# Blocked mirroring of rows, an in-place residual and a new instruction order in a linear-attention, Fourier-mixing and feed-forward kernel

## The chip, the cores and the metric

The kernel runs on one core of one Trainium2 chip. The metric is device time in microseconds (us) of one execution; less is better. TensorE is called PE below, VectorE DVE, ScalarE ACT, GpSimd POOL and SyncE SP; SP computes nothing here and only issues transfers. A time is the median of the executions listed, with the lowest and highest in brackets.

## The reference

The input is 8 batches of 8 heads, 576 rows and 64 columns per head. Each batch goes through a linear attention with exponential features, a two-dimensional Fourier transform of which the real part is kept and added, a layer norm and a feed-forward network (FFN).

```python
def phi(x):                                   # w_phi: 64 x 128
    proj = np.einsum('bhsd,df->bhsf', x, w_phi)
    proj = proj - np.max(np.abs(proj), axis=-1, keepdims=True)
    return np.concatenate([np.exp(proj), np.exp(-proj)], axis=-1)
q_p, k_p = (phi(q), phi(k))
kv = np.einsum('bhsf,bhsd->bhfd', k_p, v)
z = np.sum(k_p, axis=2)
num = np.einsum('bhsf,bhfd->bhsd', q_p, kv)
den = np.einsum('bhsf,bhf->bhs', q_p, z)[..., None] + 1e-06
# attention output num / den, heads side by side: x is (8, 576, 512)
...
mixed = np.real(np.fft.fft(np.fft.fft(x, axis=1), axis=2))
u = x + mixed
un = (u - mu) / np.sqrt(var + 1e-06)          # over the 512 columns
out = u + np.maximum(un @ w_ch1, 0.0) @ w_ch2 # 512 -> 2048 -> 512, float32
```

## The kernel before

The real part of the transform of row s and column c equals the one of the mirrored row 576 - s and the mirrored column, so the kernel computes half of the rows and adds each product twice, once mirrored. For that it keeps a batch in five row groups on the 128 partitions: groups 0 and 1 hold rows 1 to 256 in pairs, groups 2 and 3 hold rows 320 to 575 **mirrored**, and group 4 holds rows 0 and 257 to 319. The mirrored groups must be stored in reversed order of rows. Before the change, the reversal is within blocks of 64 partitions:

```python
def out_rows(b, c):
    if c < 2:
        r = out[b, 1:257, :].rearrange("(a r j) n -> a r j n", r=64, j=2)[:, :, c, :]
        return [(slice(64, 128), r[0]), (slice(0, 64), r[1])]
    r = out[b, 320:576, :].rearrange("(a r j) n -> a r j n", r=64, j=2)
    return [(slice(0, 128), r[:, ::-1, 3 - c, :])]

def forward(b):
    ...                                        # 32 steps of the first FFN matrix, then:
    for c in range(4):
        ...                                    # 16 matmuls into po
        O = outp.tile([128, C], F32, tag="O", name="O")       # two such buffers
        nc.vector.scalar_tensor_tensor(
            out=O[:], in0=po[:], scalar=rs[:, c:c + 1], in1=U[:, c, 0:C],
            op0=ALU.mult, op1=ALU.add,
        )
        for ps_, rows_ in out_rows(b, c):
            nc.sync.dma_start(out=rows_, in_=O[ps_, :])
        yield
    ...                                        # group 4: a third and a fourth use of O
```

The loads are issued from POOL, the transposes (done by transfers) and the stores from SP, one after another (in one period of the profile before, Q's transposes from 301.4 us, a store at 309.9, K's transposes at 312.4):

```python
def turn_k(KS, KS4):
    ...
    for g in range(2):
        nc.sync.dma_start_transpose(
            out=KT[:, 8 * g:8 * g + 8, :],
            in_=KS[:, 4 * g:4 * g + 4, :].rearrange("p h x -> p (h x)"),
        )
    nc.sync.dma_start_transpose(out=KT4[:], in_=KS4[:].rearrange("p h d -> p (h d)"))
    return KT, KT4

def fetch_k(b):
    turned_k[b] = turn_k(*load_k(b))           # load and transposes in one step
    yield
```

The order of instructions is written by hand as a string. Each letter takes one step of one generator: F the FFN of batch b; M, D, N the heads and mixing, folding and normalising of batch b+1; P, T, R, S query maxima, key and query features, key maxima and scaling of the values of batch b+2; K and V its loads; Q and A the load and the transposes of Q of batch b+3. A letter whose condition is not yet met is held and tried again at each later letter.

```python
PERIOD = (
    "FFMFMFPMPFMPFKMFPMPFMFFVMMMFFFTMFFFMTFFFMRFFFMFFMFFFPFMTDMFFTFSFFTFRFFFF"
    "TDFFNFRMSFFMMTFRMMSTTFFFQTFSTRFFNTFNTAFMFFFTFTFFTNFFFTTFTFNFFFF"
)
...
weave(START, P=P, T=T, R=R, S=S_)              # features of batch 0
staged[1] = load_q(1)
load_ffn_weights()
arrive_1 = arrive(1)                           # transposes of Q of batch 1
next(arrive_1)
for b in range(-1, B):
    ...
    weave(PERIOD if b >= 0 else FIRST, **streams)
```

Of the kernel before, what the change touches and what calls it, by code (L numbers as in the profile page):

```python
# [9 lines left out]
AT = mybir.ActivationFunctionType  # L10
# [10 lines left out]
START = "STTPTRTRTTSSTRTRTRPSSPTTTTPPTTTTPT"  # L21
FIRST = "MMMPMPMMPMKMMMMMPTSTTRTRSVSMTMTRPMPTTTTSMRRTTDTMNSNTQDTTNMMMMNTTMANMTTTT"
PERIOD = (
    "FFMFMFPMPFMPFKMFPMPFMFFVMMMFFFTMFFFMTFFFMRFFFMFFMFFFPFMTDMFFTFSFFTFRFFFF"
    "TDFFNFRMSFFMMTFRMMSTTFFFQTFSTRFFNTFNTAFMFFFTFTFFTNFFFTTFTFNFFFF"
)
# [8 lines left out]
def kernel(  # L35
# [10 lines left out]
    nc = tc.nc  # L46
# [21 lines left out]
    outp = ctx.enter_context(tc.tile_pool(name="outp", bufs=2))  # L68
# [21 lines left out]
    def load_ffn_weights():  # L90
        nc.gpsimd.dma_start(out=W1b[:], in_=moe_w_ch1.rearrange("(j p) h -> p j h", p=128))
        nc.gpsimd.dma_start(out=W2b[:], in_=moe_w_ch2.rearrange("(j p) c -> p j c", p=128))

# [5 lines left out]
    TURN = const.tile([128, 128], F32, name="TURN")  # L99
# [10 lines left out]
    def count():  # L110
        nc.gpsimd.iota(pc_i[:, 0:1], pattern=[[1, 1]], base=0, channel_multiplier=1)
        for g in range(2):
            nc.gpsimd.iota(
                pc_i[64 * g:64 * g + 64, 1:2], pattern=[[1, 1]],
                base=129 - 128 * g, channel_multiplier=2,
            )
        nc.gpsimd.iota(rc_i, pattern=[[1, C]], base=0, channel_multiplier=0)

    def generate_constants():
# [13 lines left out]
        for j in range(2):  # L133
            for a in range(2):
                nc.vector.tensor_scalar(
                    out=rs[:, 128 * j + 64 * a:128 * j + 64 * a + 64], in0=rc[:, 0:64],
                    scalar1=2.0, scalar2=float(129 - 128 * a + j), op0=ALU.mult, op1=ALU.add,
                )
# [32 lines left out]
    def fix_constants():  # L171
# [7 lines left out]
        tn = gi[:, 3, 0:128].bitcast(F32)  # L179
        nc.gpsimd.iota(  # L180
            rc_i[:, 0:128], pattern=[[1, 128]], base=0, channel_multiplier=1
        )
        nc.vector.tensor_copy(out=tn, in_=rc_i[:, 0:128])
        nc.vector.tensor_single_scalar(out=TURN[:], in_=tn, scalar=63.0, op=ALU.is_equal)
        nc.vector.scalar_tensor_tensor(
            out=TURN[:], in0=tn, scalar=191.0, in1=TURN[:], op0=ALU.is_equal, op1=ALU.add
        )
# [25 lines left out]
    def load_q(b):  # L213
# [3 lines left out]
        for g in range(2):  # L217
            nc.gpsimd.dma_start(
                out=QS01[64 - 64 * g:128 - 64 * g],
                in_=q[b, :, 1 + 128 * g:129 + 128 * g, :].rearrange(  # L220
                    "h (p j) d -> p h (j d)", j=2
                ),
            )
        nc.gpsimd.dma_start(
            out=QS23[:], in_=q[b, :, 320:576, :].rearrange("h (p j) d -> p h (j d)", j=2)
        )
# [44 lines left out]
    def features(b):  # L271
# [115 lines left out]
        def weigh_q():  # L387
            pt = pk.tile([128, H, 2], F32, tag="pk", name="pt")
            nc.tensor.matmul(pt[:], lhsT=TURN[:], rhs=mq[:, :, 2:4], start=True, stop=True)
            nc.scalar.activation(  # L390
                out=E2[:, :, 0:2], in_=mq[:, :, 0:2], func=AT.Exp, scale=2.0
            )
            nc.scalar.activation(
                out=E2[:, :, 4:5], in_=mq[:, :, 4:5], func=AT.Exp, scale=2.0
            )
            nc.scalar.activation(out=E2[:, :, 2:4], in_=pt[:], func=AT.Exp, scale=2.0)
# [16 lines left out]
        def queries(t, g):  # L413
            QT = (QT01, QT23)[t]
            psh = pj.tile([128, 2, 4, 128], F32, tag="pj", name="psh")
            for jj in range(2):
                rr = slice(64 * jj, 64 * jj + 64)
                rq = QT[rr, 4 * g:4 * g + 4, :]
                if t:
                    rq = rq.rearrange("p h (a r) -> p (h a) r", r=64)[:, :, ::-1]  # L420
# [228 lines left out]
    def out_rows(b, c):  # L649
        if c < 2:  # L650
            r = out[b, 1:257, :].rearrange("(a r j) n -> a r j n", r=64, j=2)[:, :, c, :]
            return [(slice(64, 128), r[0]), (slice(0, 64), r[1])]
        r = out[b, 320:576, :].rearrange("(a r j) n -> a r j n", r=64, j=2)
        return [(slice(0, 128), r[:, ::-1, 3 - c, :])]

    def forward(b):
# [15 lines left out]
        for c in range(4):  # L672
            po = pb.tile([128, C], F32, tag="pb", name="pso")
            for hh in range(NHH):
# [6 lines left out]
            O = outp.tile([128, C], F32, tag="O", name="O")  # L681
            nc.vector.scalar_tensor_tensor(  # L682
                out=O[:], in0=po[:], scalar=rs[:, c:c + 1], in1=U[:, c, 0:C],
                op0=ALU.mult, op1=ALU.add,
            )
            for ps_, rows_ in out_rows(b, c):
                nc.sync.dma_start(out=rows_, in_=O[ps_, :])
            yield
        po = pb.tile([128, C], F32, tag="pb", name="pso")
        for hh in range(NHH):  # L690
# [7 lines left out]
        O = outp.tile([128, C], F32, tag="O", name="O")  # L698
        nc.vector.scalar_tensor_tensor(
            out=O[0:64, :], in0=po[0:64, :], scalar=rs[0:64, 4:5], in1=U[0:64, 4, 0:C],  # L700
            op0=ALU.mult, op1=ALU.add,
        )
        nc.vector.scalar_tensor_tensor(
            out=O[0:64, :], in0=po[64:128, :], scalar=rs[0:64, 4:5], in1=O[0:64, :],
            op0=ALU.mult, op1=ALU.add,
        )
        nc.sync.dma_start(out=out[b, 257:320, :], in_=O[1:64, :])
        nc.sync.dma_start(out=out[b, 0:1, :], in_=O[0:1, :])
        yield


    staged = {}

    def fetch_q(b):
        staged[b] = load_q(b)
        yield

    def arrive(b):
        turned_q[b] = turn_q(*staged.pop(b))
        yield  # L720

    def fetch_k(b):
        turned_k[b] = turn_k(*load_k(b))
        yield

    def fetch_v(b):
        values[b] = load_v(b)
        yield

    def fold_later(b):  # L730
        yield from folds[b]
# [7 lines left out]

    NEEDS = {  # L740
        "D": lambda i, n: n("M") >= 15 + i,
        "M": lambda i, n: n("D") >= 2 if i >= 16 else True,
        "N": lambda i, n: n("M") >= (21, 21, 22, 22, 23, 23)[min(i, 5)],
        "T": lambda i, n: n("K") >= 1 and n("M") >= (8 if i < 9 else 16),
        "R": lambda i, n: n("T") >= (2 * i + 1 if i < 4 else 9),
        "S": lambda i, n: n("V") >= 1 and n("R") >= min(i + 1, 5) and n("M") >= 8,
        "Q": lambda i, n: True,
        "A": lambda i, n: n("Q") >= 1 and n("T") >= 18 and n("P") >= 6,
    }

    def weave(plan, **streams):
        done = {}
        live = dict(streams)

        def count_of(name):
            return done.get(name, 0) if name in streams else 1000

        def step(name):
            if name not in live:
                return True  # L760
            if name in NEEDS and not NEEDS[name](done.get(name, 0), count_of):
                return False
            try:
                next(live[name])
                done[name] = done.get(name, 0) + 1
            except StopIteration:
                del live[name]
                done[name] = 1000
            return True

        held = []
# [4 lines left out]
        while live:  # L776
            for name in list(live):
                step(name)

    with tc.manual_schedule():  # L780
        count()
        turned_k[0] = turn_k(*load_k(0))
# [57 lines left out]
```

## Time and profile before

| | before |
|---|---|
| time | 594.2 us (592.3 to 595.4) |
| span of the profiled execution | 590.6 us |
| busy: PE, DVE, ACT, POOL | 71%, 57%, 50%, 46% |
| first FFN matmul | 118.9 us |
| one period in the middle (between starts of Q's transposes) | 64.3 to 66.0 us |
| last stretch (last sum of a full row group to the end) | 12.2 us |

A period here is one batch through all stages, woven with its neighbours, so the time is about the fill plus some five periods plus the last batches, which have less and less beside them.

### The profile page before, as it was taken

The numbers are of one execution on the slowest core, as the hardware profiler recorded it, in microseconds if no ns is written. First come the engines' busy times: TensorE is split into PE (matmuls) and PEld (weight loads), VectorE is DVE, ScalarE is ACT, GpSimd is POOL, SyncE is SP. The second block draws the span as 40 slices with busy tenths as digits, with TensorE's granted clock in tenths as the row PEclk, the third lists the DMA queues.
The fourth block names the chain that finished last, engine by engine and source line by source line (L and its number), as shares of the span: only waits on it lengthen the run. The fifth ranks groups of instructions, "written<-read, shape, count | busy, mean of one in ns | idle before, by whom it ended". The sixth has DMA issues, their size and how long they took to land.

```text
span 590.6 us, 9983 instructions
## 1 busy us (share of the span) xinstructions
PE 422.1 (71%) x3881; PEld 255.2 (43%) x3904; DVE 338.5 (57%) x621; ACT 296.1 (50%) x644; POOL 273.0 (46%) x351
## 2 busy tenths in 40 slices
PE   0231442598897689759984989658967988999892
PEld 0111430177345553546443743535335734854651
DVE  7740476566766378437764577528844675557111
ACT  2771055347673468337653667336743766631520
POOL 8191079247662365518661566336651753441000
PEclk9999999989998799879998799979997899999897
DMA  9749950691199307990499009930799007006111
GB/s 115 89 43 180 191 75 0 66 150 28 21 110 152 42 9 97 143 75 2 50 136 123 15 19 105 152 48 1 93 120 111 2 22 74 27 18 70 35 36 44
DMA packets 115806, 42.66 MB, mean 72 GB/s; under 512 B 92080, under 2 KB 110640, under 8 KB 115760
## 3 DMA queue, kind: packets, MB, share of 16 engines
q1 hardware_dynamic: 63504, 23.67, 34.5%
q0 software_dynamic: 52256, 18.37, 29.0%
q8 instruction: 30, 0.49, 0.4%
q14 instruction: 16, 0.13, 0.1%
HBM read 36.77 MB, written 9.44 MB: 78 GB/s over the span
## 4 chain that ended last, share of the span: by engine, by line
DMA 32%; PE 29%; DVE 22%; POOL 6%; ACT 4%; issue 4%; SPq 2%; DVEq 0%; POOLq 0%; ACTq 0%
DMA KT<-KS 13%; DMA QT<-QS 12%; PE pso L675 10%; PE psf L663 8%; DMA out_dram<-O 4%; POOL FEO L467 3%; DVE MK L346 3%; DVE SE L480 2%; PE psD L578 2%; DVE st L628 2%; PE pu L600 2%; DVE cb L528 2%; DMA KS<-in_k_dram 2%; POOL X L531 2%; DVE MQ L383 2%
## 5 line engine op out<-in xcount | busy, mean ns | idle before, releaser
L663 PE MATMUL psf<-UT,W1b 128*128 128x288 bf16 x1024 | 158.1, 304 | 13.4 <-DMA UT<-UN 6.9
L668 ACT ACTIVATE HT<-psf 128x288 bf16<-128x288 f32 x256 | 104.4, 413 | 98.4 <-PE psf L663 90.3
L675 PE MATMUL pso<-W2b,HT 128*128 128x512 bf16 x490 | 119.8, 380 | 2.1 <-issue 1.9
L663 PEld LDWEIGHTS <-W1b 128*128 128x128 bf16 x1024 | 98.2, 104 | 45.8 <-issue 17.9
L531 POOL TENSOR_TENSOR X<-cb,rd 128x320 f32<-128x320 f32 x64 | 46.2, 722 | 151.4 <-DVE rd L530 150.8
L675 PEld LDWEIGHTS <-HT 128*128 128x128 bf16 x512 | 44.9, 98 | 55.6 <-issue 10.2
L383 DVE TENSOR_REDUCE MQ<-psq 128x8 f32<-128x1024 f32 x32 | 38.4, 1222 | 49.3 <-PE psq L376 49.3
L305 POOL TENSOR_TENSOR VCn<-VS,VCn 128x512 bf16<-128x512 bf16 x32 | 34.1, 1065 | 50.4 <-ACT VCn L301 46.6
L467 POOL TENSOR_TENSOR FEO<-X 128x320 f32<-128x320 f32 x64 | 55.4, 886 | 2.5
L330 PE MATMUL psk<-wphi,KT 64*128 64x128 bf16 x256 | 15.5, 253 | 55.0 <-DMA KT<-KS 48.5
L336 ACT ACTIVATE KPp<-psk 128x1024 bf16<-128x1024 f32 x32 | 32.9, 1029 | 43.3 <-PE psk L330 42.4
L346 DVE TENSOR_REDUCE MK<-psk 128x8 f32<-128x1024 f32 x32 | 38.7, 1210 | 18.3 <-ACT KPp L336 12.3
L376 PE MATMUL psq<-wphi,QT 64*128 64x128 bf16 x256 | 15.3, 250 | 46.2 <-DMA QT<-QS 42.3
L509 ACT CAST kvh<-kv 128x130 bf16<-128x130 f32 x64 | 17.2, 268 | 46.0 <-PE kv L505 45.0
L682 DVE SCALAR_TENSOR_TENSOR O<-pso,rs,X 128x512 f32<-128x512 f32 x32 | 23.7, 739 | 27.6 <-PE pso L675 27.6
L430 ACT ACTIVATE QPHP<-psh 128x1024 bf16<-128x1024 f32 x32 | 32.8, 1026 | 7.5 <-PE psh L421 7.5
L336 ACT ACTIVATE KPn<-psk 128x1024 bf16<-128x1024 f32 x32 | 33.1, 1035 | 6.4 <-DVE MK L346 6.4
L330 PEld LDWEIGHTS <-KT 64*128 64x128 bf16 x256 | 9.3, 108 | 61.6 <-DMA KT<-KS 50.6
L305 POOL TENSOR_TENSOR VCp<-VS,VCp 128x512 bf16<-128x512 bf16 x32 | 34.4, 1074 | 0.0
L430 ACT ACTIVATE QPHN<-psh 128x1024 bf16<-128x1024 f32 x32 | 32.8, 1026 | 0.0
L642 POOL TENSOR_SCALAR VE<-MV 128x5 f32<-128x5 f32 x8 | 4.1, 515 | 62.0 <-DVE MV L629 62.0
L376 PEld LDWEIGHTS <-QT 64*128 64x128 bf16 x256 | 8.9, 106 | 52.3 <-DMA QT<-QS 45.0
(389 smaller groups left out, 803.3 us busy)
## 6 DMA issues: line engine op xcount, KB each, us to landing
KS<-in_k_dram POOLq DMA_DIRECT2D x16, 256.0 KB, 6.7
VS<-in_v_dram POOLq DMA_DIRECT2D x8, 512.0 KB, 15.8
out_dram<-O SPq DMA_DIRECT2D x32, 128.0 KB
out_dram<-O SPq DMA_DIRECT2D x16, 256.0 KB
QS<-in_q_dram POOLq DMA_DIRECT2D x16, 128.0 KB, 3.4
QS<-in_q_dram POOLq DMA_DIRECT2D x8, 256.0 KB, 6.2
W1b<-in_moe_w_ch_dram POOLq DMA_DIRECT2D x1, 2048.0 KB, 16.1
W2b<-in_moe_w_ch_dram POOLq DMA_DIRECT2D x1, 2048.0 KB, 28.3
```

The costliest lines, as they stand in the source:

```text
L305: nc.gpsimd.tensor_tensor(out=VC[:, hs, :, 0:D], in0=values[b][0][:, hs, :].rearrange("p h (j d) -> p h j d", d=D), in1=VC[:, hs, :, D:D + ...
L330: nc.tensor.matmul(psk[:, jj, x, :], lhsT=turned_k[b][0][rr, 4 * pr + x, :], rhs=wphi2[rr, :], start=True, stop=True,)
L336: nc.scalar.activation(out=KP[:, hs, :, :].rearrange("p e (jp jj) f -> p jj (e jp) f", jj=2), in_=psk[:], func=AT.Exp, scale=sgn,)
L346: nc.vector.tensor_reduce(out=MK[:, 2 * pr:2 * pr + 2, :].rearrange("p e (jp jj) -> p jj (e jp)", jj=2), in_=tiles[pr][:], axis=AX.X, op=A ...
L376: nc.tensor.matmul(psq[:, jj, x, :], lhsT=QT[rr, 4 * g + x, :], rhs=wphi2[rr, :], start=True, stop=True,)
L383: nc.vector.tensor_reduce(out=mv_, in_=psq[:], axis=AX.X, op=ALU.max, apply_absolute_value=True)
L430: nc.scalar.activation(out=o, in_=psh[:], func=AT.Exp, scale=sgn)
L467: nc.gpsimd.tensor_tensor(out=FEO[:, :, i, a:a + D], in0=X[:, :, a:a + D], in1=X[:, :, C - a:C - a - D:-1], op=op,)
L531: nc.gpsimd.tensor_tensor(out=X[:, :, D * h:D * h + D], in0=cb[:, :, 0:D], in1=rd[:].to_broadcast([128, 5, D]), op=ALU.mult,)
L663: nc.tensor.matmul(ps[:], lhsT=W1b[:, cc, 128 * hh:128 * hh + 128], rhs=UT[:, cc, 288 * hf:288 * hf + 288], start=(cc == 0), stop=(cc == N ...
L668: nc.scalar.activation(out=HT[:, hh, 288 * hf:288 * hf + 288], in_=ps[:], func=AT.Relu)
L675: nc.tensor.matmul(po[:], lhsT=HT[:, hh, 128 * c:128 * c + 128], rhs=W2b[:, hh, :], start=(hh == 0), stop=(hh == NHH - 1),)
```

## The change

Its intent has four parts. The mirrored groups are reversed in blocks of 32 rows, so that their stores have four blocks as the outermost dimension, in place of two. The residual sum is written back over the tile X that holds it and is stored from there, so the output buffers fall away. The load of K and its transposes become two streams (K and B). And the order of all steps is new, with the start, the weights (W) and all batches in one plan, and conditions that count steps per batch.

```diff
-START = "STTPTRTRTTSSTRTRTRPSSPTTTTPPTTTTPT"
-FIRST = "MMMPMPMMPMKMMMMMPTSTTRTRSVSMTMTRPMPTTTTSMRRTTDTMNSNTQDTTNMMMMNTTMANMTTTT"
-PERIOD = (...)
+START = "TTTRTRSRTTRQSRSPTAPTTTTTPTSPPSKTTTPTMMTPMMTPWMMMPTMWTMRMTMTSPMRTTMPTMSNNDMTRPNSSMTRVRTSQBMAMMDMMTMTNTTTNTTMN"
+PERIOD = "MFMFMKRFMPVFMPFFPMFPFPMFMMFFMFMFFMTFFMFFMFBFPFFMRFFFFTFMFDFTFSSFTFSTFFFFMFQFDFFTFMFFMFRMTTFMNTTRTFFMFFFFTNFSNTTFFFRFFNATFNFTSTFFTFFNFMFFFF"
...
-    outp = ctx.enter_context(tc.tile_pool(name="outp", bufs=2))
...
-        for g in range(2):
+        for QS, at in ((QS01, 1), (QS23, 320)):
             nc.gpsimd.dma_start(
-                out=QS01[64 - 64 * g:128 - 64 * g], ...
+                out=QS[:], in_=q[b, :, at:at + 256, :].rearrange("h (p j) d -> p h (j d)", j=2)
             )
... (constants and the small product that turns the maxima, for blocks of 32)
-    def out_rows(b, c): ...
+    def store(b, U, c):
+        if c == 1:
+            for a in range(4):
+                nc.sync.dma_start(
+                    out=out[b, 193 - 64 * a:257 - 64 * a, :].rearrange("(r j) n -> r j n", j=2),
+                    in_=U[32 * a:32 * a + 32, 0:2, 0:C],
+                )
+        elif c in (2, 3):
+            rows_ = out[b, 320:576, :].rearrange("(a r j) n -> a r j n", r=32, j=2)
+            nc.sync.dma_start(out=rows_[:, ::-1, 3 - c, :], in_=U[:, c, 0:C])
...
-            O = outp.tile([128, C], F32, tag="O", name="O")
             nc.vector.scalar_tensor_tensor(
-                out=O[:], in0=po[:], scalar=rs[:, c:c + 1], in1=U[:, c, 0:C],
+                out=U[:, c, 0:C], in0=po[:], scalar=rs[:, c:c + 1], in1=U[:, c, 0:C],
                 op0=ALU.mult, op1=ALU.add,
             )
-            for ps_, rows_ in out_rows(b, c):
-                nc.sync.dma_start(out=rows_, in_=O[ps_, :])
+            store(b, U, c)
...
     def fetch_k(b):
-        turned_k[b] = turn_k(*load_k(b))
+        staged["k", b] = load_k(b)
+        yield
+
+    def arrive_k(b):
+        turned_k[b] = turn_k(*staged.pop(("k", b)))
         yield
... (conditions for every letter and batch, and one for the PSUM buffers)
```

## The prediction

> **What bounds the kernel now.** I read the page first (busy shares, the 40 slices, the chain), then who waited for whom, then one batch period in stretches with the busy time of each engine, and last the instructions around the largest holes. No engine is the bound: PE is busy 71% of the span, DVE 57%, ACT 50%, POOL 46%. The chain of work that ended last names transfers first:
>
> ```profile
> DMA 32%; PE 29%; DVE 22%; POOL 6%; ACT 4%; issue 4%; SPq 2%; DVEq 0%; POOLq 0%; ACTq 0%
> ```
>
> In the middle one batch costs about 65 us: in that chain the transposes of Q start at 171.7, 236.5, 301.4, 365.7 and 431.7 us. I cut one such period at the first matmul on the new K (columns: length, busy us and count of PE, weight loads, DVE, ACT, POOL; then clock, DMA share, GB/s):
>
> ```profile
> 301.40:326.00 24.60, 13.79 (x208) 10.01 (x206) 10.28 (x14) 8.03 (x26) 9.79 (x15) 0.90 1.35 127
> 326.00:365.70 39.70, 37.27 (x281) 20.66 (x286) 29.99 (x58) 27.73 (x54) 23.68 (x28) 0.93 0.33 42
> ```
>
> The second part is nearly full on PE (37.3 of 39.7 us); the first loses 24.6 - 13.8 = 10.8 us. The timeline inside it:
>
> ```profile
> 306.61 0.74 DVE L699 SCALAR_TENSOR_TENSOR O<-pso,rs,X 64x512 f32<-64x512 f32 x1 [4.61 <-DMA out_dram<-O]
> 312.38 10.40 SPq L250 DMA_TRANSPOSE KT<-KS  x2
> 325.92 0.61 PE L330 MATMUL psk<-wphi,KT 64*128 64x128 bf16 x8 [7.26 <-DMA KT<-KS]
> ```
>
> DVE waits 4.6 us until one of the two output tiles is stored. The stores that follow on SP's queue leave late, the K transposes behind them start at 312.4, and PE, which takes its work in order, waits 7.3 us for them. The others stand still with it, and the clock stays at half for some us afterwards:
>
> ```profile
> 320.00:324.00 4.00, 0.00 (x0) 0.00 (x0) 0.00 (x0) 0.00 (x0) 0.11 (x1) 0.65 0.53 96
> 324.00:328.00 4.00, 2.08 (x23) 1.53 (x24) 0.66 (x2) 1.02 (x1) 0.00 (x0) 0.50 0.64 54
> 328.00:332.00 4.00, 4.00 (x28) 2.83 (x27) 1.71 (x5) 2.55 (x5) 2.33 (x3) 0.57 0.00 0
> ```
>
> The same waits, summed over the run:
>
> ```profile
> PE psk L330 <- DMA KT<-KS: 48.5, 8, 15.1
> PE psq L376 <- DMA QT<-QS: 42.3, 12, 13.6
> DVE O L699 <- DMA out_dram<-O: 40.0, 8, 5.4
> ```
>
> The fill is the other large loss: the first FFN matmul starts at 121 us. In it PE waits 13.6 us at 61.5 for QT of batch 1, whose transposes were issued at 42.2, just after the weights (issued at 41.7 and 42.5):
>
> ```profile
> 52.00:56.00 4.00, 0.00 (x0) 0.00 (x0) 0.00 (x0) 0.00 (x0) 0.00 (x0) 1.00 1.06 209
> 56.00:60.00 4.00, 0.00 (x0) 0.00 (x0) 0.00 (x0) 0.00 (x0) 0.00 (x0) 1.00 1.19 187
> ```
>
> [...] The mirrored stores (row groups 2 and 3) have a slowest dimension of 2 in DRAM now, 4 after. [...] such a store of 256 KB takes 7.8 us at the very end (575.7 to 583.5), about 34 GB/s, when little else runs[...]. [...] QT in the fill, issued at 42.2 and usable only at 61.5 beside the weights, against 12.7 to 22.5 for all of Q at the start. [...]
>
> **The change, part by part.**
>
> *In-place residual.* It removes the output tiles and with them the DVE wait: 8 times, 40 us on DVE. On the path it matters at three places. Each period, SP reaches the K transposes some 4 us sooner. At the start of the last two batches PE waited 6.4 us in two waits for the buffer that this DVE step holds. At the end, the last group's sum waits from 579.1 to 583.6 us: after, it starts when its matmuls are done, at 580.2, so 3.5 us.
>
> *Blocks of 32.* [...] from about 8 to 4 to 5 us (estimate, from 7.8/2 plus a fixed part). Before, row group 3 was stored from 309.9, just ahead of the K transposes. Instructions: groups 0 and 1 go out as 4 stores, as before; Q loads are one fewer per batch (0.7 us of POOL); one more small matmul, one fewer small activation. Together under 1 us per batch and beside other work.
>
> *K as two streams, new order.* I walked both plans through their conditions. In the steady period K is loaded after FFN step 2 (before: 5), transposed at step 18, and used at once; before, its first matmul stood at step 12. Seven FFN steps (7 x 0.53 us, four matmuls of 0.13 us) and four head combinations (0.3 us each on PE) thus move in front of it, about 5 us. But the load itself is issued at about the same moment (305.4 before; POOL is free perhaps 1 us later in the new order, as the small values' product is done earlier but the normaliser later), lands 6.7 us after, and V is still loaded right behind it. So K does not come much sooner than now: the gain is that PE, DVE and ACT have other work in the meantime, [...] and that PE stays warm.
>
> Period after: first part 21 to 25 us (PE work 13.8 + 5 = 19; QT is still awaited some 2 us; I take 24), second part 39.7 - 5 (moved) - 3.5 (PE at half clock for about 7 us of work) = 31.2. That is 55, against 64.9. A check: the period from 119.1 to 171.7, where no store stands in front of the K transposes, took 52.5 us; with the 3.2 us of last FFN steps that it lacks, 55.7. I take 55.5. DVE (40.3 us) and ACT (35.8 us) fit in that.
>
> *Fill.* Q of batch 1 is now loaded early and its transposes are released by the last query step, near 42 us, while the weights stand on POOL's queue behind the last values and the load of K, at about 47 us. So the 13.6 us hole should mostly close, but the K transposes of batch 1 come to lie under the weights' transfer, until about 75 us. From there the rest of batch 1's features, bounded by ACT (keys 9.5, queries 9.4, smaller 4.6 us) and the normalising take some 29 us: first FFN matmul at 104, against 121.
>
> Sum, before then after, by the marks of the trace: to the first FFN matmul 121, 104; to the next Q transposes 50.7, 49; four periods 260, 222; to the last group of batch 5 61.4, 53; to that of batch 6 46.5, 44.5; to that of batch 7 37.4, 34.5; to the end 15.7, 12. Before: 592.7 (span 590.6, rounding); after: 519. The time is 3.2 us over the span: 522 us.
>
> **The rivals.** *The wait for K takes back the gain.* K's load starts no sooner and V's 512 KB (15.8 us to landing) still runs beside its transposes. If K lands as late as now (24.5 us into the period), only the moved work, the warm clock and the fill pay: periods of 57 to 58, total near 535. If the deeper order delays it further, 550. *The fill does not shorten*, because K or V of batch 1 now waits for the weights in place of Q: 538. *DVE and ACT chains become the bound*: DVE would be busy 40.3 of 55 us, with each head combination a chain of 1.2 us and the folding behind it on POOL; a period of 58 gives 535. *Better than I think*: if K no longer waits at all, PE's 51 us with the stretched cold part taken off leave a period near 52 to 53: about 505. *The stores are hidden anyway*: partly true in mid-period, since only the last group waits for them. Nothing in the change adds work of weight, so slower needs an unlucky new wait of 10 us per batch.
>
> **Range and chances.** The fill may give 5 to 25 us, the periods 6 to 12 each over five and a half of them, the end 5 to 9. All low: 594 - 5 - 33 - 5 = 551; all high: 594 - 25 - 66 - 9 = 494. Eight times in ten 502 to 550. Faster by over 2% 0.95, within 2% 0.03, slower 0.02.
>
> **What would show it right or wrong.** Right: distances of about 55 us between successive Q transposes; no DVE wait for the output; PE's wait for KT under 20 us in all (48.5 now); clock in mid-run above 0.95; the first FFN matmul near 104 us; store of group 2 at the end in 4 to 5 us. Wrong: K transposes still awaited 7 us per period, though the order moved; a wait for the weights or V of the same size in the fill; a DVE chain without idle time in front of PE. The step I trust least is the landing of K at 21 to 24 us into the period, then the fill.

## More of the kernel before

The prediction shows the chain, the stretches and the waits. Two views that it does not show matter later, both from the profile's summary page. The first is its part on transfer queues: packets, megabytes, and the time that the packets took, as a share of the span of 16 engines.

```profile
q1 hardware_dynamic: 63504, 23.67, 34.5%
```

By its size this queue carries what SP issues: 9.44 MB of stores, which is all that the page has as written to HBM, and by the sizes of their tiles 14.2 MB of transposes. The second is its part on transfers by issue: from what to what, issuer, count, size of each, median time from issue to landing.

```profile
KS<-in_k_dram POOLq DMA_DIRECT2D x16, 256.0 KB, 6.7
VS<-in_v_dram POOLq DMA_DIRECT2D x8, 512.0 KB, 15.8
```

## The result and the profile after

The changed kernel takes **518.6 us** (514.0 to 520.4, four executions) against 594.2 us (592.3 to 595.4, four). The ratio is 0.872, with a 95% interval from 0.866 to 0.878: faster. Ratios here are the mean time of one kernel's fast runs over that of the other's of the same rounds, so not quite the ratio of the medians quoted. The profiled execution was one with a span of 516.2 us.

The chain of work that ended last, by engine, of the changed kernel:

```profile
PE 52%; DMA 23%; DVE 13%; POOL 5%; ACT 4%; SPq 1%; issue 1%; POOLq 0%; DVEq 0%
```

PE has taken the first place from the transfers (29% before, 52% now). The waits of PE over the run, of the changed kernel (in total, times, longest, in us):

```profile
PE pm L556 <- DVE HI L488: 16.2, 8, 5.1
PE psk L327 <- DVE gt L155: 15.4, 1, 15.4
PE psq L358 <- DMA QT<-QS: 9.8, 3, 6.5
PE psk L327 <- DMA KT<-KS: 9.7, 6, 4.5
PE psq L373 <- DMA QT<-QS: 8.5, 6, 2.2
...
PE psf L670 <- DMA UT<-UN: 5.1, 2, 4.1
```

The wait for the transposed K fell from 48.5 to 9.7 us, and that for Q from 42.3 to 8.5 us, with another 9.8 us at the smaller query group. Not all of K's fall is a gain: the first wait of the run, 15.1 us, was put down to K's transposes before, and the same wait, 15.4 us, is now put down to DVE, because by the profile DVE's result came last. Counted without it, K's wait fell from 33.4 to 9.7 us (with it, to 25.1, above the 20 us that the prediction set as a sign of being right), and in the four middle periods alone from 27.0 to 2.2. The largest wait left is for DVE's folding. No wait of DVE for the output is left in the list.

One period in the middle, of the changed kernel, in the same stretches and columns as the prediction's (length; busy us and count of PE, weight loads, DVE, ACT, POOL; clock, DMA share, GB/s), then the whole period:

```profile
209.15:230.60 21.45, 18.69 (x269) 13.96 (x268) 14.77 (x28) 9.69 (x27) 11.36 (x16) 0.92 1.44 147
230.60:263.94 33.34, 31.44 (x224) 16.06 (x223) 26.25 (x45) 25.70 (x51) 22.06 (x26) 1.00 0.36 49
209.15:263.94 54.79, 50.13 (x491) 30.02 (x490) 41.01 (x72) 35.39 (x78) 33.42 (x41) 0.97 0.78 87
```

PE now stands idle for 21.45 - 18.69 = 2.8 us in the first part, against 10.8 before. Over the whole period its idle time fell from 13.2 us (64.30 - 51.07, in the same cut of before) to 4.7, its busy time from 51.1 to 50.1. So of the 9.5 us that the period lost, 8.6 were idle time of PE, and 0.9 PE's own work running faster.

Around the K wait, the timeline of that period (start, duration, engine, line, and in brackets the idle time before and what ended it):

```profile
211.48 1.67 POOL L207 DMA_DIRECT2D KS<-in_k_dram  x2
...
217.81 8.89 SPq L247 DMA_TRANSPOSE KT<-KS  x2
...
230.10 0.40 PE L327 MATMUL psk<-wphi,KT 64*128 64x128 bf16 x8 [0.57 <-DMA KT<-KS]
```

K's load is issued 2.3 us into the period (4.0 before), its transposes 8.7 us in (11.0 before), and its first matmul starts 20.95 us in (24.5 before) after a wait of 0.6 us (7.3 before). K's way is still long, as the chain of work that ended last shows in this period (start, duration, what):

```profile
211.48 6.32 DMA KS<-in_k_dram
217.81 12.25 DMA KT<-KS
```

The load and the transposes are hidden behind other work now, not gone.

The fill, from the timeline of the changed kernel:

```profile
101.29 0.65 PE L670 MATMUL psf<-UT,W1b 128*128 128x288 bf16 x4 [4.07 <-DMA UT<-UN]
```

The first FFN matmul starts at 101.3 us; before, at 118.9. (The prediction took 121 from a coarser reading; the first one in the timeline stands at 118.92.) The last row of interest is in the chain of the changed kernel (start, duration, what):

```profile
52.97 21.61 DMA KT<-KS
```

The transposes of K of batch 1 now lie under the weights, until 74.6 us, where the prediction put about 75.

Last, the two views of transfers, first the queue that SP feeds, then the loads of K and V, both of the changed kernel:

```profile
q1 hardware_dynamic: 63536, 23.67, 31.3%
```

```profile
KS<-in_k_dram POOLq DMA_DIRECT2D x16, 256.0 KB, 6.4
...
VS<-in_v_dram POOLq DMA_DIRECT2D x8, 512.0 KB, 12.8
```

The same 23.67 MB take 31.3% of 516.2 us, 161.6 us, against 34.5% of 590.6, 203.8 us. V lands in 12.8 us instead of 15.8. The change did nothing to V's loads, which is the first hint that the stores weigh on more than themselves.

### The profile page after: what moved, and what is told of

It is laid out like the page before. It is cut to its first block, busy times and chain, and to the rows that moved or that the text cites. A ratio compares the mean times of both kernels' runs of the same rounds, so it can differ in the third digit from the quotient of the medians.

```text
span 516.2 us, 9993 instructions
## 1 busy us (share of the span) xinstructions
PE 414.4 (80%) x3920; PEld 251.0 (49%) x3920; DVE 344.6 (67%) x631; ACT 293.3 (57%) x636; POOL 271.5 (53%) x346
## 3 DMA queue, kind: packets, MB, share of 16 engines
q1 hardware_dynamic: 63536, 23.67, 31.3%
## 4 chain that ended last, share of the span: by engine, by line
PE 52%; DMA 23%; DVE 13%; POOL 5%; ACT 4%; SPq 1%; issue 1%; POOLq 0%; DVEq 0%
PE pso L682 18%; PE psf L670 16%; DMA KT<-KS 13%; DMA KS<-in_k_dram 6%; PE pu L600 4%; PE psD L578 3%; POOL FEO L467 2%; DMA QT<-QS 2%; DVE HI L488 2%; DVE CEO L476 2%; PE psh L421 1%; DVE SE L480 1%; PE pso L697 1%; PE psk L327 1%; PE kv L501 1%; SPq L247 1%
## 5 line engine op out<-in xcount | busy, mean ns | idle before, releaser
L670 PE MATMUL psf<-UT,W1b 128*128 128x288 bf16 x1024 | 151.2, 291 | 5.6 <-DMA UT<-UN 5.1
L682 PE MATMUL pso<-W2b,HT 128*128 128x512 bf16 x512 | 124.1, 385 | 0.0
L670 PEld LDWEIGHTS <-W1b 128*128 128x128 bf16 x1024 | 92.7, 99 | 30.4 <-issue 7.6
L682 PEld LDWEIGHTS <-HT 128*128 128x128 bf16 x512 | 46.4, 98 | 57.3 <-issue 8.7
L467 POOL TENSOR_TENSOR FEO<-X 128x320 f32<-128x320 f32 x64 | 52.7, 844 | 2.5
L327 PE MATMUL psk<-wphi,KT 64*128 64x128 bf16 x256 | 14.0, 240 | 36.0 <-DVE gt L155 15.4
L688 DVE SCALAR_TENSOR_TENSOR X<-pso,rs,X 128x512 f32<-128x512 f32 x32 | 23.9, 745 | 28.6 <-PE pso L682 28.6
L430 ACT ACTIVATE QPHP<-psh 128x1024 bf16<-128x1024 f32 x32 | 32.8, 1024 | 10.6 <-PE psh L421 10.5
L333 ACT ACTIVATE KPp<-psk 128x1024 bf16<-128x1024 f32 x32 | 32.8, 1025 | 9.8 <-PE psk L327 9.8
L509 ACT CAST kvh<-kv 128x130 bf16<-128x130 f32 x64 | 17.2, 269 | 34.1 <-PE kv L505 33.4
L302 POOL TENSOR_TENSOR VCp<-VS,VCp 128x512 bf16<-128x512 bf16 x32 | 36.5, 1141 | 0.0
L605 DVE TENSOR_TENSOR X<-pu,X 128x512 f32<-128x512 f32 x16 | 11.0, 687 | 26.6 <-PE pu L600 26.6
L516 PEld LDWEIGHTS <-QPHP 128*128 128x128 bf16 x320 | 26.4, 104 | 3.4 <-DVE cb L528 2.1
L628 DVE BATCH_NORM_STATS2 st<-X 128x6 f32<-128x512 f32 (+1 forms) x40 | 27.4, 684 | 0.3
## 6 DMA issues: line engine op xcount, KB each, us to landing
VS<-in_v_dram POOLq DMA_DIRECT2D x8, 512.0 KB, 12.8
```

The costliest lines, as they stand in the source:

```text
L302: nc.gpsimd.tensor_tensor(out=VC[:, hs, :, 0:D], in0=values[b][0][:, hs, :].rearrange("p h (j d) -> p h j d", d=D), in1=VC[:, hs, :, D:D + ...
L327: nc.tensor.matmul(psk[:, jj, x, :], lhsT=turned_k[b][0][rr, 4 * pr + x, :], rhs=wphi2[rr, :], start=True, stop=True,)
L333: nc.scalar.activation(out=KP[:, hs, :, :].rearrange("p e (jp jj) f -> p jj (e jp) f", jj=2), in_=psk[:], func=AT.Exp, scale=sgn,)
L430: nc.scalar.activation(out=o, in_=psh[:], func=AT.Exp, scale=sgn)
L467: nc.gpsimd.tensor_tensor(out=FEO[:, :, i, a:a + D], in0=X[:, :, a:a + D], in1=X[:, :, C - a:C - a - D:-1], op=op,)
L628: nc.vector.bn_stats(out=st[0:M, :], in_=X[0:M, c, 0:C])
```

## The experiments

Twelve kernels ran, each with three timed rounds beside the kernel before, which lay at 594.1 to 595.2 us each time. All results are right unless it is said otherwise. A mirrored store is called wider here the more pieces its outermost dimension has: two before the change, four after it.

### 1. The in-place residual alone

```diff
--- before
-            O = outp.tile([128, C], F32, tag="O", name="O")
-                out=O[:], in0=po[:], ...
+                out=U[:, c, 0:C], in0=po[:], ...
-                nc.sync.dma_start(out=rows_, in_=O[ps_, :])
+                nc.sync.dma_start(out=rows_, in_=U[ps_, c, 0:C])
```

> The kernel before with the residual updated in place and stored from there, nothing else. My theory: the DVE wait for an output tile (40 us in all) goes, but the K transposes still wait for a load that is issued at the same moment, so a middle period shrinks by 1 to 2 us only (64.9 to about 63.5); with 3.8 us at the end and some 6 us at the start of the last two batches about 577 us. Rival: the output wait heads the chain of SP's queue, the K transposes start 4 us sooner in each of six periods: about 559 us. No effect (hidden): 594.

Measured: 585.3 us (583.5 to 588.6), ratio 0.986 (0.981 to 0.991), a gain that is clear of the noise but under 2%. DVE's 40 us of waits for the output are gone from the list. The four middle periods are not shorter: 63.6, 65.5, 65.4 and 66.0 us, against 64.9, 64.9, 64.3 and 66.0. The timeline of this kernel shows SP in the period that starts at 302.32:

```profile
302.32 3.40 SPq L260 DMA_TRANSPOSE QT<-QS  x1
305.83 2.40 SPq L261 DMA_TRANSPOSE QT<-QS  x1
...
313.45 11.46 SPq L249 DMA_TRANSPOSE KT<-KS  x2
```

SP reaches the K transposes 11.1 us into the period, as before (11.0). It is held not by the output buffer: from Q's first transpose on it issues almost without a gap, Q's transposes for 3.4, 2.4 and 1.2 us, the normalised rows' for 1.6 and three stores for 1.9 in all. Nor would an earlier SP have gained much, since K's load is issued 3.9 us into the period (4.0 before) and took 6.5 us to land by the median of this run, so landed at about 312.8 (an estimate), 0.7 us before the transposes start. So 40 us of waiting on DVE were worth nothing in the periods. The gain lies in the last two batches: from the last-group matmuls of batch 5 to those of batch 7 it is 74.8 us (499.3 to 574.1), 83.2 before, where two waits of PE for DVE's last sum (2.6 and 3.9 us) have gone. And the end is unchanged:

```profile
574.21 0.75 DVE L680 SCALAR_TENSOR_TENSOR X<-pso,rs,X 128x512 f32<-128x512 f32 x1 [2.70 <-PE pso L674]
576.07 1.53 DVE L697 SCALAR_TENSOR_TENSOR X<-pso,rs,X 64x512 f32<-64x512 f32 x2 [1.10 <-PE pso L690]
```

The last sum starts at once (576.07, when its matmuls end) and not after a store; still, from the sum of group 3 at 574.21 to the end at 586.5 it is 12.3 us, as before (578.37 to 590.6, 12.2). The last wait in the run is SP's, 6.7 us for a store. That this is the mirrored store after the sum of group 3 is my reading: the stores of group 4 are issued at 577.6 and 578.0 us here, 3.4 us after that sum (585.1 and 585.5 before, 6.8 after it), and the end did not move with them.

### 2. Blocks of 32 alone

Output buffers and order stay. To make room for the larger turning matrix, the float copy of w_phi, used only at the start, moved into one of the two output buffers. Groups 0 and 1 go out as eight stores.

```diff
--- before
-    TURN = const.tile([128, 128], F32, name="TURN")
+    TURN = const.tile([128, 2, 128], F32, name="TURN")
-        r = out[b, 320:576, :].rearrange("(a r j) n -> a r j n", r=64, j=2)
+        r = out[b, 320:576, :].rearrange("(a r j) n -> a r j n", r=32, j=2)
... (loads of Q, constants and groups 0 and 1 as in the change)
```

> The kernel before with blocks of 32 rows (and the output tiles kept; groups 0 and 1 need 8 smaller stores then). Theory: [...] the DVE wait for the output falls from 5 us to 1 or 2 us per batch, and the end gains 3 us: about 582 us. Rival: the transfers around the K transposes, not the output wait, gain most [...]: K transposes land 3 to 4 us sooner, under 570 us. No effect: 594.

Measured: 563.2 us (559.2 to 566.3), ratio 0.948 (0.942 to 0.953), that is 31 us. The periods are 59.6, 60.4, 61.4 and 59.0 us. PE's waits in this kernel:

```profile
PE psk L330 <- DMA KT<-KS: 38.7, 8, 14.8
PE psq L376 <- DMA QT<-QS: 27.7, 10, 12.5
```

Both fell without any change of order (48.5 and 42.3 before). From the sum of group 3 to the end it is now 8.4 us instead of 12.2, so the end's gain belongs to this part. V lands in 12.0 us. The prediction had given this part under 1 us per batch beside the shorter stores; it gives about 5.

### 3. The order and the two K streams alone

```diff
--- after
-    TURN = const.tile([128, 2, 128], F32, name="TURN")
+    TURN = const.tile([128, 128], F32, name="TURN")
... (blocks of 64, two output buffers and out_rows as before the change)
```

> The changed kernel with output tiles and blocks of 64 as before: only the new order and the two K streams. Theory: the order carries the fill (20 us) and most of each period (work moved in front of the first K matmul), while the output wait of 5 us stays in each period on DVE: periods 58 to 59 us, about 543 us. Rival: the order pays only when the stores are out of the way (period above 62 us): 565 us or more. Other rival: the order is everything: 525 or less.

Measured: 554.0 us (553.8 to 556.8), ratio 0.934 (0.930 to 0.937), that is 40 us. The first FFN matmul is at 99.9 us, so 19 us come from the fill; the periods are 62.0, 61.0, 58.8 and 61.1 us, some 4 us shorter each. The waits of PE and DVE, and V's landing, of this kernel:

```profile
PE psk L328 <- DMA KT<-KS: 25.4, 5, 14.8
...
PE psq L374 <- DMA QT<-QS: 16.1, 7, 3.6
```

```profile
DVE O L697 <- DMA out_dram<-O: 28.3, 8, 4.5
```

```profile
VS<-in_v_dram POOLq DMA_DIRECT2D x8, 512.0 KB, 16.7
```

The transfers are as slow as before the change (16.7 us for V); the order alone does not relieve them, it gives PE other work while they run. In the four middle periods PE's wait for K is nearly gone with the order alone (3.7 us, 27.0 before). What remains there is the wait for Q, 13.0 us, and 5.9 us for the normalised rows.

The three single parts give 0.986 x 0.948 x 0.934 = 0.873, and the whole change 0.872. That the product fits does not show that each part keeps its worth beside the others; the next experiment shows that one does not.

### 4. The change without the in-place residual

```diff
--- after
+    outp = ctx.enter_context(tc.tile_pool(name="outp", bufs=2))
-                out=U[:, c, 0:C], in0=po[:], ...
+                out=O[:], in0=po[:], ...
-            store(b, U, c)
+            for ps_, rows_ in out_rows(b, c):
+                nc.sync.dma_start(out=rows_, in_=O[ps_, :])
```

> The changed kernel with two output tiles again (blocks of 32 and the new order kept). Theory: [...] the wait for a tile is 1 to 2 us per batch and 2 us at the end: about 528 us. Rival: the tile wait holds SP's queue as before, 4 us per period: 545 us. Rival: nothing, as the stores are quick enough: 518.

Groups 0 and 1 go out as eight stores here, as in experiment 2, so the run differs from the change by four more stores per batch too.

Measured: 520.6 us (516.0 to 521.9), ratio 0.874 (0.869 to 0.879). The intervals of the two kernels overlap almost wholly: in the changed kernel the in-place residual is worth nothing that can be measured, though DVE waits 14.3 us for the output without it. The end is 8.45 us from the sum of group 3 (8.5 with the in-place sum). The 33 us from experiment 3 to this one are the blocks of 32 in the new order.

The four kernels with output tiles make a square: old or new order, blocks of 64 or 32. Time, and the mean of the four middle periods of the profile (us):

| | blocks of 64 | blocks of 32 |
|---|---|---|
| old order | 594.1, 65.0 | 563.2, 60.1 |
| new order | 554.0, 60.7 | 520.6, 56.2 |

The order is worth 40 us beside blocks of 64 and 43 beside blocks of 32, and 4.3 and 3.9 of it per period; the blocks are worth 31 and 33 us, and 4.9 and 4.5 per period. Within this square the two gains add up.

### 5. How much the mirrored stores cost: the kernel before with its mirrored rows stored in plain order

The rows of groups 2 and 3 are stored in plain order, so that the outermost dimension is the 128 partitions. The result is **wrong** (relative error 0.17); sizes and the number of instructions are unchanged.

```diff
--- before
-        r = out[b, 320:576, :].rearrange("(a r j) n -> a r j n", r=64, j=2)
-        return [(slice(0, 128), r[:, ::-1, 3 - c, :])]
+        r = out[b, 320:576, :].rearrange("(r j) n -> r j n", j=2)
+        return [(slice(0, 128), r[:, 3 - c, :])]
```

> The kernel before, row groups 2 and 3 stored in plain order (128 rows as the slowest dimension of the store), so 192 or so rows of each batch come out in wrong places on purpose; not one instruction is added or removed. Theory after the first runs: [...] faster than with blocks of 32 (563): about 550 us, and the PE waits for KT and QT fall by half. Rival: blocks of 32 gained by the merged load of Q or by the smaller stores: 590.

Measured: 543.9 us (541.6 to 546.4), ratio 0.915 (0.910 to 0.919): **51 us from the form of two stores per batch** (pieces and reversal together). The queue of SP, the loads, one period and SP's timeline in it, of this kernel:

```profile
q1 hardware_dynamic: 63728, 23.67, 24.5%
```

```profile
KS<-in_k_dram POOLq DMA_DIRECT2D x16, 256.0 KB, 5.8
VS<-in_v_dram POOLq DMA_DIRECT2D x8, 512.0 KB, 10.4
```

```profile
231.22:289.57 58.35, 51.38 (x490) 30.69 (x488) 40.16 (x72) 35.76 (x80) 33.48 (x42) 0.94 0.66 82
```

```profile
231.22 1.23 SPq L261 DMA_TRANSPOSE QT<-QS  x1
...
240.47 6.57 SPq L250 DMA_TRANSPOSE KT<-KS  x2
```

The same bytes take 24.5% of 544.6 us, 133 us, in place of 204. V lands in 10.4 us in place of 15.8. Q's transposes are issued in 1.2 us each (3.2 for the first one before), and K's in 6.6 us (10.4). So SP is through with the stores in front of the K transposes sooner (7.3 us into the period, 10.9 before) and then waits for K's load (13 times, 32.3 us in the run; 5 times, 19.9 us before). The transposes themselves are done sooner too: in the chain that ended last, K's took 9.2 us in this period, 13.5 in the one of before. In the four middle periods PE waits 17.0 us for K (27.0 before) and not at all for the larger Q groups (14.2 before). PE does the same work as before, 51.4 us per period. The order was not touched.

### 6. The changed kernel with wider and with narrower mirrored stores

First as in experiment 5, then with two blocks of 64, reversed within each. Both results are **wrong**; only the rows' places in the output differ.

```diff
--- after, wider
-            rows_ = out[b, 320:576, :].rearrange("(a r j) n -> a r j n", r=32, j=2)
-            nc.sync.dma_start(out=rows_[:, ::-1, 3 - c, :], in_=U[:, c, 0:C])
+            rows_ = out[b, 320:576, :].rearrange("(r j) n -> r j n", j=2)
+            nc.sync.dma_start(out=rows_[:, 3 - c, :], in_=U[:, c, 0:C])
--- after, narrower
-            rows_ = out[b, 320:576, :].rearrange("(a r j) n -> a r j n", r=32, j=2)
+            rows_ = out[b, 320:576, :].rearrange("(a r j) n -> a r j n", r=64, j=2)
```

> The changed kernel with the same plain order of stores (wrong rows on purpose)[...]. Theory: the rest of the waits for QT (18 us) and KT (10 us) is partly still the narrow store: about 508 us. Rival: [...] the stores no longer stand in the way and PE bounds the period: 518, same.

> The changed kernel with the mirrored stores written as two blocks of 64 reversed rows (wrong rows on purpose): [...] the layout, Q loads and everything else as changed. Theory: back to near the run with only the new order (554): about 548 us, periods near 60 us. Rival: [...] 525 or less.

Measured: wider 493.5 us (491.1 to 498.0), ratio 0.831 (0.824 to 0.838); narrower 558.5 us (554.6 to 560.5), ratio 0.938 (0.931 to 0.944). With two, four and 128 outermost pieces the changed kernel takes 558.5, 518.6 and 493.5 us. From two to four pieces nothing changes but the grouping of the same reversed rows, and that step is 40 us. From four to 128 the reversal goes as well, so that step of 25 us does not separate the two.

### 7. The old period in the new scheme, first attempt

```diff
--- after
-PERIOD = "MFMFMKRFMPVFMP..."
+PERIOD = "FFMFMFPMPFMPFKBMFPMPF..."     # the old one, K written as KB
```

> The changed kernel with the old order in the repeated period (K loaded and transposed at one step, as before), the new start kept. Theory: the old order with wider stores took 563; minus about 20 us of fill and a few us for the in-place sum: 540 us, periods 59 to 60. Rival: with the stores out of the way the old order of the period is as good as the new: 520.

Measured: 739.7 us (737.3 to 741.3), ratio 1.24. This is inconclusive. The old scheme let leftover steps of a period run at its end; the new one takes exactly one step per letter, and the old string is short of one F, N and S and has one T too many. The streams drift apart from batch to batch. It only shows how much an order can cost.

### 8. The old period, mended

```diff
--- experiment 7
-...TTFTFNFFFF"
+...TTFNFFFFFNS"                       # last T out, F, N and S added
```

> The changed kernel, new start kept, with the order of the repeated period as before (mended: in the first try the period lacked three steps and had one too many, so the streams drifted apart from batch to batch). Theory: [...] the old order took 563; less some 20 us of fill and under 8 us for the in-place sum: about 538 us, so the new period is worth some 20 us. Rival: with the stores out of the way the old period is as good as the new: 520.

Measured: 550.9 us (550.2 to 551.4), ratio 0.926 (0.921 to 0.930). The first FFN matmul is at 100.0 us, and the periods are 60.7, 61.9, 61.3 and 64.9 us. PE's wait for K in this kernel:

```profile
PE psk L327 <- DMA KT<-KS: 36.0, 8, 6.9
```

So with the new start, blocks of 32 and the in-place sum, the new period is 32 us quicker than this mended one, or some 7 per period (a mean of 62.2 against 54.9), and the wait for K is where it shows: 22.2 us of it in the four middle periods, 2.2 in the changed kernel. That is more than the 4 us per period in the square of experiment 4, but it is not the worth of the new order: the old order as it really ran, beside blocks of 32 and even with the output tiles (experiment 2), had periods of 60.1 us, so a part of the 7 belongs to the mended string.

### 9. The old start in the new scheme

```diff
--- after
-START = "TTTRTRSRTTRQSRSPTAPTTTTT..."
+START = "STTPTRTRTTSSTRTRTRPSSPTTTTPPTTTTPTQWWAMMMPMP..."
```

> The changed kernel with the start's order as before (Q of batch 1 and the weights loaded together, then its transposes), the new period kept. Theory: the fill costs what it did, first FFN matmul near 120 us in place of 101: about 538 us. Rival: the start is repaired by wider stores or the later steps: 522 or less.

Measured: 630.8 us (626.1 to 631.3), ratio 1.058. The total is inconclusive: four surplus T of the old start stay pending and fire early in every later period. The fill comes before that and can be read, in the timeline and in the chain of this kernel:

```profile
117.03 1.12 PE L670 MATMUL psf<-UT,W1b 128*128 128x288 bf16 x4 [6.41 <-DMA UT<-UN]
```

```profile
43.73 22.45 DMA QT<-QS
```

With the old start the first FFN matmul is at 117.0 us, with the new one at 101.3, and the 22 us under the weights are Q's again. The fill's gain, some 16 us, is the order of the start.

### 10. Blocks of 16

If four pieces are better than two, eight might be better than four, with right results. Groups 0 and 1 then need eight stores of 16 partitions each.

```diff
--- after
-            for a in range(4):
+            for a in range(8):
                 nc.sync.dma_start(
-                    in_=U[32 * a:32 * a + 32, 0:2, 0:C],
+                    in_=U[16 * a:16 * a + 16, 0:2, 0:C],
-            rows_ = out[b, 320:576, :].rearrange("(a r j) n -> a r j n", r=32, j=2)
+            rows_ = out[b, 320:576, :].rearrange("(a r j) n -> a r j n", r=16, j=2)
... (constants for blocks of 16)
```

> The changed kernel with mirrored blocks of 16 rows in place of 32, results right: [...] row groups 0 and 1 in eight stores of 64 KB in place of four of 128 KB. Theory: [...] about 506 us. Rival: the four additional stores on SP's queue delay the transposes behind them: 516 or more.

The expected 506 us lie between the times with four pieces and with 128 (experiment 6). Measured: 534.5 us (531.6 to 537.4), ratio 0.899 (0.893 to 0.905): 16 us slower than the changed kernel, where I had expected it faster. A wait of PE, and SP's stores of groups 0 and 1, in this kernel:

```profile
PE psq L382 <- DMA QT<-QS: 29.9, 10, 5.4
```

```profile
261.82 5.15 SPq L661 DMA_DIRECT2D out_dram<-X  x8
```

The wait for Q stands at 29.9 us (8.5 in the changed kernel) and that for K lies wholly in the fill, the eight stores keep SP for 5.2 us in place of 2.6 for four, V lands in 14.1 us (12.8) and the periods are 58 to 62 us. Two things changed at once, the mirrored stores with eight pieces and the plain ones cut into sixteen partitions, and this run does not tell which of them costs. That stays open.

### 11. Blocks of 16, with K loaded half a period earlier

The letter K moves beside Q, and B behind step 8 of T of the batch before.

```diff
--- blocks of 16
-PERIOD = "MFMFMKRFMPVFM...FFMFBFPFFMR...FMFQFDFF...NTTRTFFMFF..."
+PERIOD = "MFMFMRFMPVFM...FFMFTFPFFMR...FMFKQFDFF...NTTRTBFFMFF..."
... (a few T shifted; K and B at the end of START)
```

> Blocks of 16 as in the run before, and K loaded half a period earlier, beside Q's load, and transposed as soon as the last key step of the batch before has read the buffer; its first matmul stays where it is. Theory: K's load and transposes leave the stretch where Q's transposes and V's load run, PE waits neither for KT nor long for QT, periods 51 to 52 us: about 492 us. Rival: K now collides with Q's load, the normalised rows' transposes and the stores of groups 0 and 1, and nothing is won: 506.

Measured: 558.8 us (557.5 to 564.5), ratio 0.941 (0.935 to 0.948), 24 us slower than experiment 10. After the fill PE waits for K in neither of the two kernels, so there was nothing to win, and much to lose: PE's wait for Q is 32.8 us in 7 times, and that for the normalised rows 15.9 us; Q's two larger transposes are issued in 1.8 to 5.7 us each. That the earlier load slows the transposes beside which it now runs is my reading; no run separates it.

### What could not be tried

Three kernels were to store the mirrored groups with the reversed rows as the outermost dimension, one store per block, with right results. They did not compile and never ran. No version found beats the changed kernel with right results; 493.5 us with rows in the wrong order is an estimate of what a wider mirrored store could still bring, about 25 us.

## Why the prediction was right or wrong

The time was predicted as 522 us, and measured as 518.6, well in the range; the period as 55.5 us, and measured as 54.9 (mean of 55.0, 54.8, 54.4 and 55.4). By the prediction's own stages, from the traces (us):

| stretch | before | predicted | after |
|---|---|---|---|
| to the first FFN matmul | 118.9 | 104 | 101.3 |
| to the next Q transposes | 52.8 | 49 | 52.9 |
| four periods | 260.0 | 222 | 219.6 |
| to the last group of batch 5 | 63.4 | | 58.7 |
| to that of batch 6 | 45.8 | | 42.3 |
| to that of batch 7 | 37.3 | | 32.9 |
| to the end | 12.3 | | 8.6 |

For the last four rows the prediction used somewhat earlier marks, so its savings are compared: it took 8.4, 2.0, 2.9 and 3.7 us, and the traces have 4.7, 3.6, 4.4 and 3.7. The missed part in the first of them is one wait of 6.5 us for the smaller Q group, seen in the one profiled execution. The 3.2 us that the prediction adds from the span to the time set the median beside the span of one execution; that execution took 592.4 us, 1.8 over its span.

**That the sum came out is in part luck.** Its period gives the whole 9.4 us to the order and under 1 us to the blocks. In the square of experiment 4 the order has 3.9 to 4.3 us and the blocks 4.5 to 4.9, and about 1.3 are left for the in-place sum (56.2 against 54.9, one profile each). Two wrong shares made a right period. The check behind it may have carried the missing share without saying so: it used the one period of the kernel before that had no store in front of the K transposes, 52.5 us against 65.

**The in-place residual: "Each period, SP reaches the K transposes some 4 us sooner" failed.** Experiment 1 removed DVE's wait and SP came to the K transposes at 11.1 us, as before. A wait of 40 us on DVE, read from the profile correctly, was not on the path: SP was busy with the issue of Q's transposes and what follows them, and K's load would not have landed much sooner. The piece at the last two batches held (6.4 us predicted, 8.4 measured in the profile of experiment 1). The piece at the end failed too: "it starts when its matmuls are done" came true, and won nothing, because by my reading the store behind group 3 ends the run. The end's 3.7 us came true in size because the blocks of 32 shortened that tail from 12.2 to 8.4 us.

**Blocks of 32: the term that was mis-sized.** The prediction gave this part "under 1 us per batch" in instructions, and looked only at how soon the store itself is done. It is worth 31 us alone, some 5 per period, and 33 to 40 us in the new order. Its own store was mis-sized a little as well: 4 to 5 us predicted, and in experiment 4, where DVE waits for it, 6.0 us (from the end of the sum at 508.95 to 514.97 us), against 7.9 before. That four pieces in place of two would halve it was the estimate, and what sets the time of such a store was not shown. The times of the kernel at two, four and 128 pieces (558.5, 518.6 and 493.5 us) fall as the pieces rise; the 534.5 us at eight pieces (experiment 10) do not fit in, with smaller plain stores beside them. What was missing is that the store slows what runs beside it. That it does is shown: experiment 5 changed the form of two stores per batch (pieces and reversal) and nothing else, and V's load (15.8 to 10.4 us), K's load (6.7 to 5.8), K's transposes (13.5 to 9.2 in a middle period) and their issue on SP (10.4 to 6.6) all became quicker. How it does was not shown, neither for the loads, which POOL issues, nor for the transposes, which SP issues like the stores. This also explains why the rival "the stores are hidden anyway" fell: the stores are hidden, and what they delay is not.

**The order: right in its path, too large in its share.** The wait for K went as forecast, with the order alone (3.7 us in four periods). But the order alone left the wait for Q and brought 4.3 us per period, not 9.4. In the changed kernel the two parts of the period missed in opposite directions. The work moved in front of the K matmuls was put at 5 us of PE; PE's busy time in the first part rose from 13.8 to 18.7, 4.9 us. K's first matmul was put at 24 us into the period and stands at 20.95, because K's load is issued 1.6 us earlier and not 1 us later, its transposes start 6.3 us after that (7.0 before), and they take 12.25 us (13.5). Against that, the second part was to shrink to 31.2 us and is 33.3: of "PE at half clock for about 7 us of work", worth 3.5 us, only 0.9 us showed as shorter busy time. In the period of before the clock is recorded at 0.50 from about 321.2 to 331.3 us, and PE works in 5.4 us of that; in the changed kernel it is recorded at 0.50 from about 214.9 to 218.3 us, now in the first part, and PE works all through it. So some 5.4 us of work at half clock became 3.5, worth about 1 us (an estimate from these stretches). The mean clock of the period rose from 0.92 to 0.97, more by the idle stretch at 0.50 that went (4.7 us) than by the work at 0.50 that became less (1.9 us). (That the prediction's views record the clock at 1.00 from 52 to 60 us, with PE idle, does not show that PE was quick after it: see the last section.)

**The fill: right.** 17 us predicted and 17.6 measured; experiment 9 ties some 16 of it to the start's order, and the K transposes under the weights until 75 us came as described.

**The rivals.** "The wait for K takes back the gain" was the most likely alternative. It fell: with the new order the wait is nearly gone, with the wider stores (2.2 us in four periods, 27.0 before) and without them (3.7, experiment 3). Without the wider stores the periods would have been 59 to 62 us all the same, but for Q and the normalised rows, which this rival did not name. "DVE and ACT chains become the bound" fell; PE is busy 50.1 of 54.8 us. "Better than I think" came nearest to the changed kernel with wider stores, 493.5 us. "The fill does not shorten" fell.

## What to carry to other kernels

Here the stores whose outermost dimension is only 2 slowed the transfers beside them: V's load, itself unchanged, landed in 14.2 to 16.7 us beside them (the kernel before and experiments 1 and 3), in 12.0 to 13.3 beside four pieces (the changed kernel and experiments 2, 4, 8 and 9) and in 10.4 beside 128 without the reversal (experiment 5), and the step from two pieces to four was worth 40 us in the changed kernel. So judge the form of a transfer by what lands later because of it, and not by whether anything waits for it. A long wait on an engine is worth its length only if what it holds back is on the path: removing 40 us of DVE's waits here gave some 9 us, and removing 14 us of them in the changed kernel nothing that can be measured. And when a sum of several parts comes out right, test the parts: here the order and the blocks each brought half of what the prediction gave to the order, which only a square of four kernels shows.

## What else the runs and traces show

- Two narrow stores per batch cost 51 of 594 us (with their reversal; from two pieces to four alone 40 us, in the changed kernel); V's load, itself unchanged, landed in 15.8 us beside them and in 10.4 without.
- A step towards more pieces, eight with smaller plain stores, was slower than four (534.5 against 518.6 us, with V landing in 14.1 against 12.8), for a reason not settled.
- SP's time to issue one and the same transpose is not constant: Q's first one in a middle period took 3.19 us in the kernel before and 1.23 us in experiment 5, where only the form of the mirrored stores differs.
- The recorded clock and the pace of PE can differ. In the kernel before, the record reads 1.00 from 52 to 60 us while PE did nothing; the eight query matmuls at 61.47 us, still recorded at 1.00, took 0.61 us together, as eight of the same size for K at 325.92 did at a recorded 0.50, where those at 312.84 took 0.40 at 1.00. So PE was slow there and the record did not show it; early in a run, check the recorded clock against the duration of equal matmuls.
